# The two heads of a pair as two 64-column products on the two halves of TensorE's array

## The chip, the cores and the metric

The kernel runs on one core of a Trainium2 chip. The metric is the device time of one execution, in microseconds (us). Before the change it is 762.14 us, the median of three runs (761.79, 762.14 and 766.78).

## The reference

Eight sequences of 576 tokens, eight heads of 64 channels each (512 channels), everything in float32:

```python
kv  = einsum('bhsd,bhse->bhde', k, v)          # per head: 64 x 64, summed over 576 tokens
out = einsum('bhsd,bhde->bhse', q, kv)
x   = out / sqrt(mean(out * out) + 1e-6) * g_norm            # heads side by side: [8, 576, 512]
gate = sigmoid(causal convolution of x over 5 tokens)
y1  = (gate * (x @ w_val)) @ w_out
theta = y1 @ w_theta
y   = w_tok_r @ (y1 * cos(theta)) + w_tok_i @ (y1 * sin(theta))
u   = y1 + y
result = u + maximum(u @ w_ch, 0)
```

The change concerns the first line alone: the product of keys and values of each head.

## The kernel before, in words

Work runs in two phases. In the first one the eight sequences go through attention, normalization, convolution and the products with w_val and w_out; in the second one through the angles, the mix over the tokens and the product with w_ch. The big products of both run as three passes over split operands; the products of attention run in plain float32, and the trace shows each such product as two MATMUL instructions with a weight load (LDWEIGHTS) each.

Heads are handled in pairs, four pairs (NP) to a sequence. A pair's keys and values lie in one tile `kv`: 128 tokens on the partitions, five chunks of tokens, 128 columns (head 0, then head 1). The fifth chunk has only 64 tokens, so it fills partitions 0 to 63. Five such buffers exist. `load_kv` issues two DMAs for each, the first four chunks and the 64 tokens of the fifth (lines 143 and 144), on the queue of SyncE (SP), which also issues the other loads of this phase.

`key_value` (line 156) multiplies keys and values of whole pairs: five products of 128 by 128 columns for a pair, added up in a PSUM bank `kvp` (line 162). Of each 128 x 128 result only the two 64 x 64 blocks on the diagonal, one for each head, are wanted; two copies on ScalarE (lines 166 and 167) take them to `bd`, which holds zeros elsewhere. `attention` (line 169) multiplies queries with `bd` (`o`, line 177), sums squares on ScalarE and VectorE (lines 180 to 186), takes the inverse root by Newton steps on VectorE (193 to 199) and scales (`xn`, line 203). `transposes` brings the result to channels over tokens (`xt`, line 218; copies on ScalarE in lines 220 and 221, the low part `xl` on VectorE in line 222), `value` multiplies by w_val (`v`, lines 238 to 240) and by the gate (`g`, `gh`, `gl`), `first` by w_out (`y`, the same lines). `conv` (line 225) is the convolution, on VectorE for the most part. Weights that arrive as doubles are decoded on VectorE and ScalarE (lines 92 to 96) where there is room.

The order of the program text gives priorities to a scheduler, which sets the order of instructions on each engine before the run: an instruction is placed when its operands are due by the scheduler's own reckoning. On the chip each engine then works through its list in that order. From the second sequence on, three pairs of heads (four in one case) of later sequences are multiplied between the end of one sequence's `v` and the next one's transposes (table UNITS, lines 36 and 359 to 372). The first loads of all are in the order of the table START (line 32), as far as the scheduler keeps to it.

Of the kernel before, what the change touches and what calls it, by code (L numbers as in the profile page):

```python
# [12 lines left out]
AF = mybir.ActivationFunctionType  # L13
ALU = mybir.AluOpType

P = 128
B = 8
S = 576
D = 64
DM = 512  # L20
NP = 4          # pairs of heads = chunks of 128 channels
NM = 4
HS = 288        # half of a sequence
PAD = 4
# [5 lines left out]
NBD = 4  # L30
# the order of the first loads: k = keys and values, q = queries (of a pair of heads), v = w_val, o = w_out, c = conv
START = "v0 k0 k1 v1 k2 k3 v2 q0 q1 q2 q3 v3 k4 c0 k5 k6 o0 k7 o1 o2 o3 q4 q5 q6 q7"
WVFIRST = 3      # chunks of w_val decoded before the first normalization
WOFIRST = 2      # chunks of w_out decoded before the second one
LEAD = 3         # sequences whose k^T v runs ahead
UNITS = (0, 3, 3, 3, 3, 4, 0, 0, 0)    # pairs of heads of later ones, with each sequence
YFIRST = 2       # chunks of the first sequence's product with w_out ahead of the second's transposes
EARLY = 2        # chunks of the convolution that run before the gate's product
RATE = (1, 3)    # chunks of weights decoded with a sequence
LATER = 1000     # their priority  # L40
CHFIRST = 2      # chunks of w_ch decoded in the first phase
MIXES = ((8,), (2, 6))      # tiles of the mix that share its stationary operands: first sequence, others
SUMS_ON_VECTOR = (range(5), (2, 4), ())
# the high word of 2**-127 as a double, read as a float32, squared
TINY = (2.0 ** -15 * 1.125) ** 2
# [3 lines left out]
def attention_moe_holo_kernel(ctx, tc, kvm, kvt, qt, gn, w_val, conv_w, w_out, w_th, w_tok, w_ch, outT):  # L49
    """x = rmsnorm(q (k^T v)) g; y1 = (sigmoid(conv x) * (x w_val)) w_out;  # L50
    u = y1 + Wr (y1 cos) + Wi (y1 sin); out = u + relu(u w_ch).

    The weights come as doubles (raw words) and are cut to float32 on the chip. Big products
    run as three float32r passes over exact 12+12-bit parts of both operands."""
    nc = tc.nc
# [9 lines left out]
    def parts(h, l, src):  # L65
        """h + l = src, both exact in float32r."""
        one = nc.scalar.activation(h, src, AF.Copy)  # L67
        return nc.vector.tensor_tensor(l, src, h.bitcast(F32), ALU.subtract), one

    def fetch(pool, src, width, name, tag=""):  # L70
        words = 1 if src.dtype == F32 else 2
        if pool is px:
            raw = pool.tile([P, width if tag else DM, words], I32, tag="raw" + tag, bufs=1 if tag else 3, name=f"raw_{name}")
        else:
            raw = pool.tile([P, DM, words], I32, tag="fT", bufs=2, name=f"raw_{name}")
        raw = raw[:, :width, :]
        # a queue of its own for the one that must not wait behind the loads of the second phase
        queue = nc.gpsimd if pool is not px else nc.sync
        if words == 1:
            raw = raw.bitcast(F32).rearrange("p a w -> p (a w)")  # L80
            queue.dma_start(out=raw, in_=src)
        else:
            queue.dma_start(out=raw, in_=src.bitcast(I32).rearrange("p (a w) -> p a w", w=2))
        return raw

    def decode(pool, raw, width, name, tag=""):
        """Doubles to float32 (toward zero; under 2**-127 to zero)."""
        if raw.dtype == F32:
            return raw
        dst = pool.tile([P, width if tag else DM], F32, tag="dst" + tag if pool is px else "fTt", bufs=(1 if tag else 2) if pool is px else 1, name=f"dst_{name}")[:, :width]  # L90
        lo, hi, d = raw[:, :width, 0], raw[:, :width, 1], dst.bitcast(I32)
        nc.vector.tensor_scalar(d, hi, 0x07FFFFFF, 3, ALU.bitwise_and, ALU.logical_shift_left)
        nc.vector.scalar_tensor_tensor(d, hi, -0x40000000, d, ALU.bitwise_and, ALU.bitwise_or)
        nc.vector.scalar_tensor_tensor(d, lo, 29, d, ALU.logical_shift_right, ALU.bitwise_or)
        nc.scalar.activation(hi.bitcast(F32), hi.bitcast(F32), AF.Square)
        nc.vector.scalar_tensor_tensor(dst, hi.bitcast(F32), TINY, dst, ALU.is_ge, ALU.mult)
        return dst
# [20 lines left out]
    nc.gpsimd.memset(halfpi, 0.5 * math.pi)  # L118
    nc.scalar.activation(halfpi, halfpi, AF.Sigmoid)      # the table of the first phase, early
    nc.gpsimd.memset(halfpi, 0.5 * math.pi)  # L120
# [7 lines left out]

    # ---------------------------------------------------------------- phase 1
    px_stack, py_stack = ExitStack(), ExitStack()  # L130
# [7 lines left out]

    def load_kv(b, pairs=range(NP)):
        kv = []  # L140
        for p in pairs:
            t = px.tile([P, 2, 5, P], F32, tag="kv", bufs=5, name=f"kv{b}_{p}")
            nc.sync.dma_start(out=t[:, :, 0:4, :], in_=kvm[b, p])
            nc.sync.dma_start(out=t[0:D, :, 4, :], in_=kvt[b, p])
            kv.append(t)
        return kv
# [9 lines left out]
    def key_value(b, kv, p0=0):  # L156
        """k^T v of the pairs from p0 on, as blocks on a diagonal"""
        ps = bank(f"kvp{b}_{p0}")
        n = len(kv)
        for p in range(n):  # L160
            for c, (_, r) in enumerate(CH):
                nc.tensor.matmul(ps[:, p * P:(p + 1) * P], kv[p][:r, 0, c, :], kv[p][:r, 1, c, :],  # L162
                                 start=(c == 0), stop=(c == 4))
        bd = bds[b % NBD]
        psv = ps.rearrange("p (a e) -> p a e", a=NP)
        nc.scalar.activation(bd[0:D, p0:p0 + n, 0:D], psv[0:D, :n, 0:D], AF.Copy)
        nc.scalar.activation(bd[D:P, p0:p0 + n, D:P], psv[D:P, :n, D:P], AF.Copy)

    def attention(b, q):
        bd = bds[b % NBD]  # L170
# [3 lines left out]
        for c, (s0, n) in enumerate(CH):  # L174
# [12 lines left out]
            po.append(o)  # L187
        # 1 / sqrt(mean + eps): an estimate from the bits, then three Newton steps
        ssf = ss.rearrange("p c h -> p (c h)")
# [76 lines left out]
    def to_tokens(rows, src, tag, bufs, name):  # L266
        """src: channels (32 i + c, m) over tokens; to rows of tokens, channels in the order (i, m, c)."""
        n = rows.shape[0] // 32
        t = qx.tile([P, n, P], F32, tag=tag, bufs=bufs, name=name)
        for v, (a, w) in src:  # L270
            nc.vector.transpose(t[:, a:a + w // 32, :].rearrange("p j (m c) -> p j m c", m=NM),
                                v.rearrange("p m (j c) -> p j m c", c=32))
        dst = rows.rearrange("(j r) (i x) -> i r j x", r=32, i=4)
        for i in range(4):
            nc.sync.dma_start(out=dst[i], in_=t[32 * i:32 * (i + 1)])
# [16 lines left out]
    def load_tails(b):  # L292
        """The last 64 tokens of two sequences."""
        ft = qx.tile([P, NM, 2, D], F32, tag="ft", bufs=1, name=f"ft{b}")
        for j in range(2):
            nc.sync.dma_start(out=ft[:, :, j, :], in_=ydram[b + j][:, :, DM:S])
        to_tokens(stdram[b // 2], [(ft[:, :, j, :], (2 * j, D)) for j in range(2)], "fTt", 1, f"fTt{b}")
        th = qx.tile([P, NM, P], F32R, tag="th", bufs=1, name=f"th{b}")
        tl = qx.tile([P, NM, P], F32R, tag="tl", bufs=1, name=f"tl{b}")
        parts(th, tl, ft.rearrange("p m j s -> p m (j s)"))  # L300
        yts = []
        for j in range(2):
            t = qx.tile([P, S], F32, tag="tok", bufs=2, name=f"ytt{b}_{j}")[:, :DM]
            for r in range(2):
                nc.sync.dma_start(out=t[r * D:(r + 1) * D], in_=stdram[b // 2][j * D:(j + 1) * D, :])
            yts.append(t)
        return th, tl, yts
# [4 lines left out]
    raw = {}  # L312
# [80 lines left out]

    # ---------------------------------------------------------------- phase 2

# [7 lines left out]
    def theta(name, yh, yl):  # L403
        """f = theta / 2 pi less its nearest integer, and |f|"""
        ps = bank(f"th{name}")
# [33 lines left out]
    def phase_tails(b, th, tl, yts):  # L439
        """Rows 0-63 hold y1 cos, rows 64-127 y1 sin, of a sequence's last 64 tokens."""  # L440
        fr, co = theta(f"t{b}", th, tl)
# [37 lines left out]
    def halves(b, then=None):  # L479
        """z of sequence b"""  # L480
        nonlocal tls, zt
# [78 lines left out]
```

## Time and profile before

| | |
|---|---|
| median of three runs | 762.14 us |
| span of the profiled execution, first to last instruction | 760.7 us |
| TensorE matmul (PE) busy | 743.6 us, 98% of the span |
| TensorE weight loads (PEld) busy | 712.0 us, 94% |
| VectorE (DVE) | 535.2 us, 70% |
| ScalarE (ACT) | 391.6 us, 51% |
| GpSimd (POOL) | 6.6 us, 1% |
| line 162, the product of keys and values | 320 matmuls, 51.3 us busy, first at 8.1 us, last at 252.8 us |

No time of its own is listed for the profiled execution; its span lies 1.4 us under the median of the runs. Times in the rows are microseconds from the start of the span, durations too unless they say ns. A matmul's duration holds its way through the array, so matmuls overlap: the pace of TensorE is read from the distance between starts, not from durations. `L162` is line 162 of the kernel before. Granted clock 1.00 is TensorE's upper level (2.4 GHz), 0.50 its lower one (1.2 GHz).

### The profile page before, as it was taken

To read this page: it belongs to the slowest core of one execution; us is meant where nothing else is said; L and a number is where in the kernel's file an instruction comes from. 1 tells how busy PE (TensorE), PEld (TensorE's weight loads), DVE (VectorE), ACT (ScalarE), POOL (GpSimd) and SP (SyncE) were. 2 spreads that over 40 slices of the span, in tenths; PEclk is the share of its full clock that TensorE was granted. 3 is DMA by queue.
4 is the path that set the end of the run, shared out by engine and by line. 5 is a ranking of instruction groups with operands and counts; after the bars stand their busy time and mean duration, and the time that the engine had idled before them with its cause. 6 is when DMAs were issued, how large, how long until landed. Compare 5 with 4: busy or idle time off the path is not lost.

```text
span 760.7 us, 13908 instructions
## 1 busy us (share of the span) xinstructions
PE 743.6 (98%) x5264; PEld 712.0 (94%) x5264; DVE 535.2 (70%) x1045; ACT 391.6 (51%) x1173; POOL 6.6 (1%) x32
## 2 busy tenths in 40 slices
PE   5899999999999999999999999999999999999998
PEld 4789999999999999989899899899999999998997
DVE  4898897979798889868883772953863934836504
ACT  2565968777777677467441550631631613614301
POOL 1000000000000000000000000000000000000000
PEclk9999999999999999999999999999999999999999
DMA  9969635545444034743527034063042161160101
GB/s 300 313 202 272 217 117 171 166 164 175 169 136 150 32 105 126 216 133 97 164 75 217 1 120 117 9 173 110 17 142 79 57 167 55 55 173 9 63 2 62
DMA packets 77539, 97.53 MB, mean 128 GB/s; under 512 B 11168, under 2 KB 50208, under 8 KB 77472
## 3 DMA queue, kind: packets, MB, share of 16 engines
q1 hardware_dynamic: 76896, 94.55, 40.5%
q0 software_dynamic: 576, 2.10, 0.8%
q8 instruction: 41, 0.67, 0.4%
q14 instruction: 26, 0.21, 0.1%
HBM read 65.66 MB, written 30.97 MB: 127 GB/s over the span
## 4 chain that ended last, share of the span: by engine, by line
PE 94%; ACT 2%; DMA 2%; DVE 1%; SPq 1%; issue 0%; DVEq 0%; ACTq 0%
PE u L461 10%; PE u L463 10%; PE u L462 10%; PE kvp L162 5%; PE y L238 5%; PE v L238 5%; PE y L239 5%; PE v L239 4%; PE y L240 4%; PE c L238 4%; PE c L240 4%; PE c L239 4%; PE v L240 4%; PE o L177 4%; PE th L409 3%; PE th L408 3%
## 5 line engine op out<-in xcount | busy, mean ns | idle before, releaser
L466 DVE TENSOR_TENSOR f<-u,f 128x288 f32<-128x288 f32 x64 | 26.5, 454 | 128.1 <-PE u L463 128.1
L67 ACT ACTIVATE uh<-f 128x288 fp32r<-128x288 f32 x64 | 26.2, 444 | 150.4 <-DVE f L466 150.4
L229 DVE SCALAR_TENSOR_TENSOR acc<-x,cw,acc 128x576 f32<-128x576 f32 x128 | 95.7, 812 | 3.2 <-ACT acc L227 3.2
L238 PE MATMUL y<-gh,woh 128*128 128x288 f32 x256 | 76.3, 299 | 0.0
L238 PE MATMUL v<-xh,wvh 128*128 128x288 f32 x256 | 76.3, 299 | 0.0
L239 PE MATMUL v<-xh,wvl 128*128 128x288 f32 x256 | 75.7, 296 | 0.0
L239 PE MATMUL y<-gh,wol 128*128 128x288 f32 x256 | 75.6, 296 | 0.0
L238 PE MATMUL c<-uh,wch 128*128 128x288 f32 x256 | 75.4, 295 | 0.0
L240 PE MATMUL c<-ul,wch 128*128 128x288 f32 x256 | 75.4, 295 | 0.0
L239 PE MATMUL c<-uh,wcl 128*128 128x288 f32 x256 | 75.4, 294 | 0.0
L240 PE MATMUL v<-xl,wvh 128*128 128x288 f32 x256 | 75.3, 294 | 0.0
L240 PE MATMUL y<-gl,woh 128*128 128x288 f32 x256 | 75.0, 294 | 0.0
L162 PE MATMUL kvp<-kv 128*128 128x128 f32 (+1 forms) x320 | 51.3, 304 | 10.1 <-DMA kv<-in_kvm_dram 8.7
L162 PEld LDWEIGHTS kvp<-kv 128*128 128x128 f32 (+1 forms) x320 | 43.3, 201 | 17.2 <-DMA kv<-in_kvm_dram 9.8
L185 ACT ACTIVATE junk<-o 128x64 f32<-128x64 f32 (+1 forms) x264 | 55.0, 250 | 4.4 <-PE o L177 3.8
L185 ACT ACTIVATION_READ_ACCUMULATOR junk<-o 128x1 f32 (+1 forms) x264 | 53.8, 233 | 0.0
L409 PE MATMUL th<-wth,yl 128*128 128x512 f32 x128 | 50.2, 393 | 0.0
L407 PE MATMUL th<-wth,yh 128*128 128x512 f32 x128 | 50.1, 391 | 0.0
L408 PE MATMUL th<-wtl,yh 128*128 128x512 f32 x128 | 50.0, 391 | 0.0
L238 PEld LDWEIGHTS v<-xh,wvh 128*128 128x128 f32 x256 | 48.0, 188 | 1.1 <-ACT junk L185 0.9
L238 PEld LDWEIGHTS y<-gh,woh 128*128 128x128 f32 x256 | 48.0, 188 | 0.7
L239 PEld LDWEIGHTS c<-uh,wcl 128*128 128x128 f32 x256 | 48.0, 188 | 0.3
(188 smaller groups left out, 2146.5 us busy)
## 6 DMA issues: line engine op xcount, KB each, us to landing
kv<-in_kvm_dram SPq DMA_DIRECT2D x32, 512.0 KB, 6.6
q<-in_qt_dram SPq DMA_DIRECT2D x32, 288.0 KB, 5.3
yd<-yo SPq DMA_DIRECT2D x64, 144.0 KB, 1.8
f<-yd SPq DMA_DIRECT2D x32, 288.0 KB, 3.8
out_dram<-f SPq DMA_DIRECT2D x64, 144.0 KB, 1.8
sd<-fT SPq DMA_DIRECT2D x64, 128.0 KB, 2.5
yt<-sd SPq DMA_DIRECT2D x8, 1024.0 KB, 5.4
raw_tk<-in_w_tok_dram SPq DMA_DIRECT2D x10, 512.0 KB, 6.2
```

Of the source, the lines that this page charges most:

```text
L162: nc.tensor.matmul(ps[:, p * P:(p + 1) * P], kv[p][:r, 0, c, :], kv[p][:r, 1, c, :], start=(c == 0), stop=(c == 4))
L185: nc.scalar.activation(junk[:n], o[:n, h * D:(h + 1) * D], AF.Square, scale=0.125, accum_out=ss[:n, c, h:h + 1])
L229: nc.vector.scalar_tensor_tensor(a, x[:, m, k:k + S], cw[:, m * 5 + k:m * 5 + k + 1], a, ALU.mult, ALU.add)
L238: nc.tensor.matmul(ps[:, :HS], wh[:, m, ks], xh[:, k, tsl], start=(k == 0), stop=False)
L239: nc.tensor.matmul(ps[:, :HS], wl[:, m, ks], xh[:, k, tsl], start=False, stop=False)
L240: nc.tensor.matmul(ps[:, :HS], wh[:, m, ks], xl[:, k, tsl], start=False, stop=(k == 3))
L407: nc.tensor.matmul(ps, yh[:, k, :], wth[0][:, k, :], start=(k == 0), stop=False)
L408: nc.tensor.matmul(ps, yh[:, k, :], wth[1][:, k, :], start=False, stop=False)
L409: nc.tensor.matmul(ps, yl[:, k, :], wth[0][:, k, :], start=False, stop=(k == 3))
L461: nc.tensor.matmul(ps[:, :HS], zh[:, ms], wkh[:, j, sl], start=(i == 0), stop=False)
L462: nc.tensor.matmul(ps[:, :HS], zh[:, ms], wkl[:, j, sl], start=False, stop=False)
L463: nc.tensor.matmul(ps[:, :HS], zl[:, ms], wkh[:, j, sl], start=False, stop=(i == 8))
```

## The change

Each chunk of tokens now gives two products instead of one: 64 columns of head 0's keys with 64 columns of its values, placed on columns 0 to 63 of the array, and the same of head 1 on columns 64 to 127 (`tile_position`). The results lie in 64 partitions each, side by side, and only the wanted blocks are computed. Partitions 64 to 127 of the fifth chunk are filled with zeros by GpSimd ahead of the loads, in every use of a buffer, and the fifth chunk is multiplied over all 128 rows. So 160 products (320 matmul instructions) of 128 x 128 columns become 320 products (640 instructions) of 64 x 64 columns, and 32 fills of 64 partitions x 256 elements are added. The copies to `bd` read the new places. Other lines of the diff only drop comments; line numbers move by one from line 143 on and by four from line 169 on.

```diff
@@ def load_kv @@
             t = px.tile([P, 2, 5, P], F32, tag="kv", bufs=5, name=f"kv{b}_{p}")
+            nc.gpsimd.memset(t[D:P, :, 4, :], 0.0)
             nc.sync.dma_start(out=t[:, :, 0:4, :], in_=kvm[b, p])
             nc.sync.dma_start(out=t[0:D, :, 4, :], in_=kvt[b, p])
...
@@ def key_value @@
         for p in range(n):
-            for c, (_, r) in enumerate(CH):
-                nc.tensor.matmul(ps[:, p * P:(p + 1) * P], kv[p][:r, 0, c, :], kv[p][:r, 1, c, :],
-                                 start=(c == 0), stop=(c == 4))
+            for c in range(5):
+                for j in range(2):
...
+                    js = slice(j * D, (j + 1) * D)
+                    nc.tensor.matmul(ps[js, p * D:(p + 1) * D], kv[p][:, 0, c, js], kv[p][:, 1, c, js],
+                                     start=(c == 0), stop=(c == 4), tile_position=(0, j * D))
         bd = bds[b % NBD]
-        psv = ps.rearrange("p (a e) -> p a e", a=NP)
-        nc.scalar.activation(bd[0:D, p0:p0 + n, 0:D], psv[0:D, :n, 0:D], AF.Copy)
-        nc.scalar.activation(bd[D:P, p0:p0 + n, D:P], psv[D:P, :n, D:P], AF.Copy)
+        psv = ps[:, 0:n * D].rearrange("p (a e) -> p a e", a=n)
+        nc.scalar.activation(bd[0:D, p0:p0 + n, 0:D], psv[0:D], AF.Copy)
+        nc.scalar.activation(bd[D:P, p0:p0 + n, D:P], psv[D:P], AF.Copy)
```

The scheduler places some work anew. The first place is the start of the program on SP's queue; `raw_wv` are chunks of w_val, `kv_0` to `kv_3` the first sequence's pairs of heads, `q_0` to `q_3` its queries. Before:

```order
L83 DMA raw_wv_117<-in_w_val_dram 128x1024
L143 DMA kv_0_119<-in_kvm_dram 128x2x512
...
L143 DMA kv_1_122<-in_kvm_dram 128x2x512
...
L83 DMA raw_wv_125<-in_w_val_dram 128x1024
L143 DMA kv_2_127<-in_kvm_dram 128x2x512
...
L143 DMA kv_3_130<-in_kvm_dram 128x2x512
...
L83 DMA raw_wv_133<-in_w_val_dram 128x1024
L152 DMA q_0_135<-in_qt_dram 128x576
L152 DMA q_1_137<-in_qt_dram 128x576
L152 DMA q_2_139<-in_qt_dram 128x576
L152 DMA q_3_141<-in_qt_dram 128x576
```

With the change:

```order
L83 DMA raw_wv_117<-in_w_val_dram 128x1024
L144 DMA kv_0_119<-in_kvm_dram 128x2x512
...
L83 DMA raw_wv_127<-in_w_val_dram 128x1024
L83 DMA raw_wv_137<-in_w_val_dram 128x1024
L153 DMA q_0_139<-in_qt_dram 128x576
L153 DMA q_1_141<-in_qt_dram 128x576
L153 DMA q_2_143<-in_qt_dram 128x576
L144 DMA kv_1_123<-in_kvm_dram 128x2x512
...
L144 DMA kv_2_129<-in_kvm_dram 128x2x512
...
L144 DMA kv_3_133<-in_kvm_dram 128x2x512
...
L153 DMA q_3_145<-in_qt_dram 128x576
```

Three of the first sequence's four pairs of heads are now asked for behind the second and third chunk of w_val and three of the queries.

The second place is TensorE where the third and fourth sequence's products of keys and values are spread over the first one's product with w_out (`y`). Before, the fourth sequence's first pair is followed by ten rows of `y`:

```order
L162 MATMUL kvp_0_700<-kv_0_571 128x128 x5
L238 MATMUL y_0_0_723<-gh_399,woh 128x288
L239 MATMUL y_0_0_723<-gh_399,wol 128x288
L240 MATMUL y_0_0_723<-gl_400,woh 128x288
...
L238 MATMUL y_0_0_723<-gh_399,woh 128x288
L162 MATMUL kvp_0_700<-kv_1_574 128x128 x5
```

With the change, by two:

```order
L166 MATMUL kvp_0_779<-kv_0_623 64x64 x10
L242 MATMUL y_0_0_822<-gh_451,woh 128x288
L242 MATMUL y_0_1_838<-gh_451,woh 128x288
L166 MATMUL kvp_0_779<-kv_1_627 64x64 x10
L243 MATMUL y_0_0_822<-gh_451,wol 128x288
```

The second pair's product has moved up by eight rows of `y`; the third and fourth pair's stand a few rows later than before. In the first sequence's `o` TensorE now goes chunk by chunk of tokens, where it went query by query. From the second sequence on the three pairs stand where they stood, behind the last row of `v` and ahead of the transposes.

## Rows read from the trace of the kernel before

**Rows 1.** Section 1 of the page: busy time, share of the span, instructions.
```profile
PE 743.6 (98%) x5264; PEld 712.0 (94%) x5264; DVE 535.2 (70%) x1045; ACT 391.6 (51%) x1173; POOL 6.6 (1%) x32
```

**Rows 2.** Section 4 of the page: the chain that ended last, shares by engine.
```profile
PE 94%; ACT 2%; DMA 2%; DVE 1%; SPq 1%; issue 0%; DVEq 0%; ACTq 0%
```

**Rows 3.** Timeline, PE, two later stretches: start, length, line, output<-input, shape, count.
```profile
98.81 4.48 PE L162 MATMUL kvp<-kv 128*128 128x128 f32 x30
103.21 2.36 PE L218 MATMUL xt<-ident,xn 128*128 128x128 f32 x20
...
247.07 5.98 PE L162 MATMUL kvp<-kv 128*128 128x128 f32 x40
252.98 2.36 PE L218 MATMUL xt<-ident,xn 128*128 128x128 f32 x20
```

**Rows 4.** Timeline, weight loads, single ones of the first of these blocks.
```profile
98.81 0.19 PEld L162 LDWEIGHTS kvp<-kv 128*128 128x128 f32 x1
...
99.48 0.19 PEld L162 LDWEIGHTS kvp<-kv 128*128 128x128 f32 x1
...
99.79 0.18 PEld L162 LDWEIGHTS kvp<-kv 64*128 64x128 f32 x1
...
100.20 0.19 PEld L162 LDWEIGHTS kvp<-kv 128*128 128x128 f32 x1
```

**Rows 5.** Timeline, weight loads of 64 columns (o), and of 64-row transposes (xt).
```profile
84.63 0.19 PEld L177 LDWEIGHTS o<-bd,q 128*128 128x128 f32 x1
84.94 0.13 PEld L177 LDWEIGHTS o<-bd,q 128*64 128x64 f32 x1
85.00 0.14 PEld L177 LDWEIGHTS o<-bd,q 128*64 128x64 f32 x1
...
85.65 0.14 PEld L177 LDWEIGHTS o<-bd,q 128*64 128x64 f32 x1
85.96 0.19 PEld L238 LDWEIGHTS v<-xh,wvh 128*128 128x128 f32 x1 [0.17 <-issue]
...
105.11 0.32 PEld L218 LDWEIGHTS xt<-ident,xn 64*128 64x128 f32 x4 [0.17 <-issue]
```

**Rows 6.** Timeline, PE and DVE, the start of the program.
```profile
15.17 1.57 PE L162 MATMUL kvp<-kv 128*128 128x128 f32 x10 [0.26 <-DMA kv<-in_kvm_dram]
17.71 4.83 PE L177 MATMUL o<-bd,q 128*128 128x128 f32 x40 [0.96 <-ACT bd L167]
...
21.51 3.05 DVE L181 TENSOR_REDUCE ss<-sq 128x8 f32<-128x512 f32 x5 [0.90 <-ACT sq L180]
...
27.30 3.08 DVE L203 TENSOR_TENSOR xn<-o,y 128x512 f32<-128x512 f32 x5
...
28.14 1.50 PE L218 MATMUL xt<-ident,xn 128*128 128x128 f32 x9 [1.99 <-DVE xn L203]
...
33.74 0.40 PE L238 MATMUL v<-xh,wvh 128*128 128x288 f32 x1
```

**Rows 7.** Windows: stretch, length, busy time by engine, granted clock, DMA share, GB/s.
```profile
12.54:17.70 5.16, 3.80 (x24) 2.88 (x24) 3.32 (x6) 2.06 (x4) 0.00 (x0) 1.00 1.04 360
29.61:33.02 3.41, 3.41 (x16) 2.96 (x15) 3.41 (x7) 1.79 (x4) 0.00 (x0) 0.50 1.01 342
```

**Rows 8.** Timeline, PE and DVE, the last early pair; the second sequence's normalization and transposes.
```profile
67.89 1.47 PE L162 MATMUL kvp<-kv 128*128 128x128 f32 x10
...
70.23 3.08 DVE L203 TENSOR_TENSOR xn<-o,y 128x512 f32<-128x512 f32 x5
...
72.58 2.30 PE L218 MATMUL xt<-ident,xn 128*128 128x128 f32 x20
```

**Rows 9.** DVE in later sequences: timeline row; waits from 112 to 223 us (total, times, longest).
```profile
99.47 3.07 DVE L203 TENSOR_TENSOR xn<-o,y 128x512 f32<-128x512 f32 x5
...
DVE g L251 <- PE v L240: 7.4, 6, 1.6
```

**Rows 10.** Timeline, POOL: a fill of 128 x 512 elements.
```profile
0.91 0.52 POOL L136 MEMSET bd<- 128x512 f32 x1
```

## The prediction

> **What bounds the kernel now.** I read the shares of busy time first, then the chain of waits, then single starts in the timeline. TensorE is busy for 98% of the span [rows 1] and holds 94% of the chain that ended last [rows 2]: what TensorE is spared, the program is spared, wherever nothing else is late in its place. So the question is what a block of key-value products takes on TensorE, read from starts. A block of three pairs begins at 98.81 and the transposes behind it at 103.21: 4.40 us for 30 instructions; the one of four pairs takes 252.98 - 247.07 = 5.91 us for 40 [rows 3]. There are four blocks of three pairs and one of four between 75 and 255 us: 4 x 4.40 + 5.91 = 23.5 us for 16 of the 32 pairs. The other 16 lie before 75 us, where other things set the pace (below).
>
> **What is in a block.** Between 98.81 and 99.48 lie six loads' steps, 0.11 us each [rows 4]: a 128-column load, beside the running product. The fifth chunk breaks the step. From the last load over 128 rows to the first over 64 it is 0.31 us, and from that, two instructions on, to the next over 128 rows 0.41 us instead of 0.22 [rows 4]. So a 64-row product costs about 0.39 us over its plain step; 4.40 is 30 x 0.11 = 3.35 and three times 0.35, in agreement. The array empties before it is used in another shape.
>
> **The change, part by part.**
>
> *The zero fill* removes that: all products run over 128 rows, so about 0.35 us a pair goes.
>
> *Entering and leaving the 64-column shape* comes in its place, once a block. The last tokens' `o` are such products now: from the last 128-column load to the first of 64 columns 0.31 us (84.63 to 84.94), and at the way out again 0.31 (85.65 to 85.96), where 0.11 is plain [rows 5]. Two changes of shape at 0.20: 0.40 us a block.
>
> *The products.* 60 instructions in place of 30 in a block of three. A 64-column load is followed by the next after 0.055 us (84.94 to 85.00), and four 64-column transposes with their loads start 0.06 us apart (the fourth load ends 0.32 after the first began, and one lasts 0.14) [rows 5]. So one after the other an instruction takes about 0.058 us. If the two halves of the array work at once, two fit into that time: 0.029. No row shows two products at once, so these are my two ends, and a third, slow one is below. I take 0.029, and this is the choice on which the forecast hangs. The reason is how loads wait in the rows: a load begins the moment the product before it begins (a load and a product both at 98.81) [rows 3, 4], which reads as waiting until the cells' spare weights have been taken over. For the other half of the columns these are other cells, whose spare weights are free a step earlier; the data moves through other columns; and the shape stays the same, so nothing need empty. Row for row the nearest value is 0.058, which is why the other case keeps a good third of the chances.
>
> With 0.029 a block of three takes 0.40 + 60 x 0.029 = 2.14 us, one of four 0.40 + 80 x 0.029 = 2.72; together 11.3 in place of 23.5: **-12.2 us**. With 0.058: 3.88 and 5.04, together 20.6: -2.9 us.
>
> The Trainium skill ("TensorEngine Tiling (Array Packing)", Tiling Modes, Key Properties) says that a change of the tiling mode drains the array but a change of tile does not, and that tiles can load and multiply in parallel; the drain agrees with 0.31 us in [rows 5], the parallel work no row here shows. By it the sum would be the -12.2 us.
>
> *What becomes late instead.* With a block of 2.14 us the transposes come at about 101.0 instead of 103.2. They need `xn`, five instructions from 99.47 to 102.54, one every 0.61 us [rows 9]: the first four are ready when their transposes (0.45 us a chunk) come, the fifth just so. VectorE's slack in a sequence is what it waits for TensorE's `v`: 7.4 us in three sequences, 2.5 each [rows 9], against 2.3 us saved in each. That is nearly all of it, so I give back a tenth: **+1.2 us**.
>
> *The start.* Behind the new order of loads the first sequence's last pair lands later: ahead of it now also stand one chunk of w_val (512 KB) and three queries (288 KB each), 1.4 MB, at 360 GB/s [rows 7] 3.9 us. It landed for 15.17; now about 19, and `o` starts at 21.6 instead of 17.71, because its operand needs all four pairs. `o` takes 4.8 us, then come the sums (five, last done at 24.56), the root, `xn` at 27.30 and the transposes at 28.14 [rows 6]. Since `o` now comes chunk by chunk, its last sum ends about 0.7 us sooner after it, so `xn` moves by some 3.2 us. Of that about 1.4 us comes back: before, a pair's product stands between the transposes, at the granted clock of 0.50 [rows 7], and makes 5.6 us of the way from the first transpose to `v` (28.14 to 33.74) [rows 6]; now the transposes follow each other. This leaves about 1.8. Against this, TensorE's 16 early pairs get shorter too, but this stretch hardly gains: the next transposes start at 72.58 and their `xn` run from 70.23 to 73.31, so at most a microsecond can come off there [rows 8]; and the fourth sequence's second pair, moved up by eight rows of `y`, makes TensorE wait for that load with `y` behind it. Idle time may also cost the clock: after the wait ahead of 28.14 the granted clock falls to 0.50 for 3.4 us [rows 6, 7], and a longer pause between loads can do this ahead of `o`, up to 2 us. Altogether **+1.5 us**, between 0 and 4.5.
>
> *The fills* cost nothing: a fill twice as wide over twice the partitions takes 0.52 us on GpSimd [rows 10], which is idle for 99% of the span [rows 1]. Each stands between a buffer's release and its DMA; in later sequences loads have a whole sequence's time ((247.07 - 98.81) / 4 = 37.07 us from one block to the next [rows 3]), which covers it. Without that cover, at most 0.5 us for each of the three pairs loaded just ahead of their use there, the last at 67.89 [rows 8], inside the +1.5. The copies to `bd` keep size and number.
>
> **Sum.** -12.2 + 1.2 + 1.5 = -9.5 us. The profiled execution's span is 760.7 us, 1.4 under the median of 762.1; against the median: 752.6, I say **753 us**.
>
> **Rivals.**
>
> *One after the other* (the change does not do what it says: the halves take turns). For it: every product in the rows starts a step after the one before, and each instruction's load is put behind the product before it. -2.9 + 1.5 gives 760.7, 757 to 766 with the start's bounds. Chance 0.34, cases in between included.
>
> *Loads no longer hidden.* If the load for one half may not run beside a product on the other half, an instruction takes load and product in turn, 0.055 + 0.058 = 0.113 us. A block of three takes 0.40 + 60 x 0.113 = 7.2 us, one of four 9.4: 38.2 in place of 23.5, +14.7; the third and fourth sequence's 8 pairs, the last at 67.89 [rows 8], add 0.8 each, of which half may hide, +3; with the start +1.5: 781 us. It decides against the change from about half of each load uncovered on (320 instructions x 0.03 = 9.6, which beats the 2.9). Against it: in [rows 5] loads of 64 columns do run beside the product on the same columns. The Trainium skill ("TensorE: Matmul & The Clock Gate", Part 3, What overlaps and what doesn't) has such a rule: loads overlap running products only on other row groups, and here both halves use all rows. By that rule the change would be slower; the 0.11 us steps in [rows 4], with all rows on both sides, do not bear it out. Chance 0.10.
>
> *Each change of half empties the array*, as each change of shape does. Then 30 changes x 0.20 come to a block of three and 40 to the one of four: 16 pairs x 10 x 0.20 = 32 over the -2.9, some 8 more before 75 us: about 800 us. Chance 0.06.
>
> **Range and chances.** The forecast, chance 0.50, runs from 748 (no slack lost, start at 0 and a microsecond gained at 72 us) to 758 (0.035 an instruction, start +4.5). With the second case the range is 748 to 768; the slow cases, 0.16, and a little at the edges stay out. A measurement of this kernel tells about 1% (7.6 us) from no change. The forecast lies just beyond it: of its 0.50 I count 0.34 as faster and 0.16 as same; of the second case 0.02 faster, 0.30 same, 0.02 slower; the slow cases slower. Faster 0.36, same 0.46, slower 0.18.
>
> **What would show it.** In the timeline, the block behind the second sequence's `v` from its first product to the transposes: 2.1 us is the forecast, 3.9 taking turns, 7 loads uncovered, 10 emptying at each change. Starts of products on the two halves nearly together in pairs would show them at once. No break of 0.3 us should be left inside a block, and one at either end. At the start `o` should begin near 21.6 and the transposes near 31. The period from block to block, 37 us now, should fall to 34.8; if the block shrinks but the period does not, VectorE is the bound and the wait of the transposes names `xn`. The forecast is wrong above all if the two halves share what a load or a product needs.

## The result, and the profile after

The change takes 755.45 us (median of four runs, 754.04 to 757.18); the kernel before, run beside it, 762.91 (four runs, 761.79 to 766.78). The ratio is 0.9888, its 95% interval 0.9857 to 0.9919: 1.1% faster, 7.5 us. The forecast was 753.

The profiled execution of the change took 757.18 us with a span of 755.4, so it is the slowest of the four. Against the profiled execution of before (span 760.7) it gains 5.3 us. They fall into three stretches, cut at the first later block of key-value products and at the transposes behind the last one:

| stretch | before | change | difference | forecast |
|---|---|---|---|---|
| start to the first later block | 98.81 | 104.60 | +5.8 | +1.5 |
| from there to the transposes behind the last block | 154.17 | 142.39 | -11.8 | -11.0 |
| from there to the end | 507.7 | 508.4 | +0.7 | 0 |

The page of the change, shares of busy time (section 1) and its chain of waits by engine (section 4):

```profile
PE 726.1 (96%) x5584; PEld 697.9 (92%) x5584; DVE 534.8 (71%) x1045; ACT 391.7 (52%) x1173; POOL 16.4 (2%) x64
...
PE 88%; DMA 4%; ACT 4%; DVE 3%; issue 0%; SPq 0%; POOL 0%; DVEq 0%; ACTq 0%; POOLq 0%
```

TensorE has 320 instructions more and is busy for 17.5 us less than in [rows 1]. Only 5.3 of them reach the span, and TensorE's share of the chain falls from 94% [rows 2] to 88%: the rest became waiting, for DMAs, ScalarE and VectorE.

The later blocks of the change, timeline of PE:

```profile
104.60 1.97 PE L166 MATMUL kvp<-kv 128*64 128x64 f32 x60
106.67 2.90 PE L222 MATMUL xt<-ident,xn 128*128 128x128 f32 x20
...
139.97 1.97 PE L166 MATMUL kvp<-kv 128*64 128x64 f32 x60
141.87 2.35 PE L222 MATMUL xt<-ident,xn 128*128 128x128 f32 x20
...
244.51 2.55 PE L166 MATMUL kvp<-kv 128*64 128x64 f32 x80
246.99 2.36 PE L222 MATMUL xt<-ident,xn 128*128 128x128 f32 x20
```

From a block's first product to the transposes it now takes 2.07 us once and 1.90 three times, where it took 4.40 [rows 3], and 2.48 in place of 5.91 for four pairs. The period from block to block is 35.4, 34.6, 35.0 and 35.0 us, where it was 37.07.

The same line, seen through four short windows that open at 104.65 and close at 104.70, 104.75, 104.81 and 104.87. A row's count is of the products that have begun by the window's end:

```profile
104.60 0.28 PE L166 MATMUL kvp<-kv 128*64 128x64 f32 x2
...
104.60 0.34 PE L166 MATMUL kvp<-kv 128*64 128x64 f32 x4
...
104.60 0.39 PE L166 MATMUL kvp<-kv 128*64 128x64 f32 x6
...
104.60 0.45 PE L166 MATMUL kvp<-kv 128*64 128x64 f32 x8
```

Two more products for each step of 0.058 us: they begin in pairs. The starts in the trace read 104.706 and 104.712, 104.764 and 104.771, 104.822 and 104.829, and so on through the block: 6 to 7 ns apart, then the next pair.

The start of the program of the change, timeline of PE, DVE and POOL:

```profile
3.83 1.58 POOL L143 MEMSET kv<- 64x256 f32 x5
...
15.13 1.34 PE L166 MATMUL kvp<-kv 128*64 128x64 f32 x20 [7.08 <-DMA kv<-in_kvm_dram]
...
21.20 6.70 PE L181 MATMUL o<-bd,q 128*128 128x128 f32 x39 [0.93 <-ACT bd L171]
...
32.20 3.07 DVE L207 TENSOR_TENSOR xn<-o,y 128x512 f32<-128x512 f32 x5
...
32.95 4.29 PE L222 MATMUL xt<-ident,xn 128*128 128x128 f32 x20 [3.20 <-DVE xn L207]
...
70.90 0.80 PE L166 MATMUL kvp<-kv 128*64 128x64 f32 x20
...
77.78 2.75 PE L222 MATMUL xt<-ident,xn 128*128 128x128 f32 x20 [1.77 <-DVE xn L207]
```

And two of its stretches (length, busy time by engine, granted clock, DMA share, GB/s):

```profile
32.15:42.39 10.24, 9.44 (x56) 8.88 (x57) 8.97 (x16) 7.34 (x14) 0.31 (x1) 0.50 0.35 131
...
66.28:69.69 3.41, 3.41 (x16) 3.41 (x15) 2.02 (x7) 0.41 (x2) 0.41 (x2) 0.50 0.94 320
```

In [rows 6] `o` takes 4.83 us; here 6.70. A pair's products take 1.34 us before 20 us and 0.80 at 70.90. At 32.15, in the wait of 3.20 us ahead of the transposes, the granted clock falls to 0.50 and stays there for 10.24 us; before the change it was 3.41 us [rows 7]. At 66.28 it falls again.

### The profile page after: what moved, and what is told of

It reads as the page before. It is cut to its first block, busy times and chain, and to the rows that moved or that the text cites. A ratio compares the mean times of both kernels' runs of the same rounds, so it can differ in the third digit from the quotient of the medians.

```text
span 755.4 us, 14634 instructions
## 1 busy us (share of the span) xinstructions
PE 726.1 (96%) x5584; PEld 697.9 (92%) x5584; DVE 534.8 (71%) x1045; ACT 391.7 (52%) x1173; POOL 16.4 (2%) x64
## 4 chain that ended last, share of the span: by engine, by line
PE 88%; DMA 4%; ACT 4%; DVE 3%; issue 0%; SPq 0%; POOL 0%; DVEq 0%; ACTq 0%; POOLq 0%
PE u L467 10%; PE u L466 10%; PE u L465 10%; PE c L244 4%; PE c L242 4%; PE c L243 4%; PE v L242 4%; PE y L242 4%; PE o L181 4%; PE v L243 4%; PE y L243 4%; PE v L244 4%; PE y L244 4%; PE th L413 3%; PE th L411 3%; PE th L412 3%
## 5 line engine op out<-in xcount | busy, mean ns | idle before, releaser
L243 PEld LDWEIGHTS v<-xh,wvl 128*128 128x128 f32 x256 | 48.9, 191 | 0.0
L243 PEld LDWEIGHTS y<-gh,wol 128*128 128x128 f32 x256 | 48.8, 191 | 0.1
L244 PEld LDWEIGHTS v<-xl,wvh 128*128 128x128 f32 x256 | 48.8, 191 | 0.0
```

Of the source, the lines that this page charges most:

```text
L243: nc.tensor.matmul(ps[:, :HS], wl[:, m, ks], xh[:, k, tsl], start=False, stop=False)
L244: nc.tensor.matmul(ps[:, :HS], wh[:, m, ks], xl[:, k, tsl], start=False, stop=(k == 3))
```

## Experiments

Times are medians; each ratio is to the kernel before as it ran beside that kernel (median 762.91 us beside the change, 763.3 beside the next four, 763.67 beside the last four). "Later block" is the start of the first one in the profiled execution. The profiled execution is not always the typical one: that of the change is the slowest of its four (757.18 us), that of the halves without fill the fastest of its four (753.42).

| kernel | us | ratio, 95% interval | later block | a block of three |
|---|---|---|---|---|
| the change | 755.45 | 0.9888, 0.9857 to 0.9919 | 104.60 | 1.90 |
| fill behind the DMAs | 753.36 | 0.9854, 0.9829 to 0.9879 | 101.01 | 1.90 |
| before, with the new order of loads | 767.11 | 1.0040, 1.0018 to 1.0061 | 102.60 | 4.40 |
| halves in turn | 758.69 | 0.9933, 0.9907 to 0.9959 | 103.56 | 2.75 |
| fill only, full products | 757.25 | 0.9906, 0.9882 to 0.9931 | 99.33 | 3.35 |
| halves, no fill | 755.55 | 0.9906, 0.9883 to 0.9928 | 97.87 | 2.63 |
| full products early | 751.37 | 0.9839, 0.9824 to 0.9854 | 99.50 | 2.18 |
| change and extra products | 759.42 | 0.9944, 0.9932 to 0.9957 | 106.80 | 1.90 |
| full early, fill behind the DMAs | 748.66 | 0.9801, 0.9787 to 0.9815 | 97.39 | 1.90 |

The block of three is the first one in the profiled execution; for the change, whose first took 2.07 us, one of the other three. The 2.18 us of full products early hold a wait for `xn`.

### Do the two halves work at once?

Halves in turn: all chunks of one head, then all of the other.

```diff
-            for c in range(5):
-                for j in range(2):
+            for j in range(2):
+                for c in range(5):
```

> The change with the loops over halves and chunks exchanged: all five chunks of head 0, then all five of head 1, so ten instructions in a row go to one half of the array. Theory (the halves work at once only because their instructions alternate; instructions begin in order): 0.058 us an instruction, a block of three pairs 3.7 to 3.9 us, some 9 to 10 us over the change: 764 to 766 us. Rival (each half has a queue of its own that runs far ahead): the block stays at 1.9 to 2.1 us and the time at 754 to 757.

Measured: a block of 2.75 us, four pairs 3.56, which neither theory gave; the time, 758.69 us, lies between theirs too. The block of this kernel, then windows that open at 103.65 and close at 103.955, 104.07, 104.18, 104.24 and 104.35 (timeline, PE):

```profile
103.56 2.82 PE L166 MATMUL kvp<-kv 128*64 128x64 f32 x60
106.31 2.36 PE L222 MATMUL xt<-ident,xn 128*128 128x128 f32 x20
...
103.56 0.56 PE L166 MATMUL kvp<-kv 128*64 128x64 f32 x6
...
103.56 0.68 PE L166 MATMUL kvp<-kv 128*64 128x64 f32 x9
...
103.56 0.80 PE L166 MATMUL kvp<-kv 128*64 128x64 f32 x13
...
103.56 0.85 PE L166 MATMUL kvp<-kv 128*64 128x64 f32 x14
...
103.56 0.97 PE L166 MATMUL kvp<-kv 128*64 128x64 f32 x16
```

Up to 103.955 one product starts per 0.058 us; then about two (9 to 13 within 0.11 us); then one again (14 to 16 within 0.11). A head has ten instructions here. So within a half the step is 0.058, and around each change of half some three instructions of the next one run beside the last of this one. The two ends of the forecast, 0.058 and 0.029, stand side by side in one block, and what decides between them is whether a product for the other half lies near enough in the queue. The instruction that signals a pair's end, by the program text its 20th, is the 23rd to start: the next pair's first ones have passed it.

The Trainium skill ("TensorEngine Tiling (Array Packing)", Tiling Modes, Key Properties) says that tiles load and multiply in parallel; starts 6 to 7 ns apart in the change agree. The Trainium skill ("TensorE: Matmul & The Clock Gate", Part 3, The mechanism) says in its list of what overlaps that loads overlap products only on other row groups and that products start in program order; the change's pairs, each on all 128 rows, and the 23rd start here do not bear either out.

### What are the fill and the split worth apart?

Fill only: the change with one 128 x 128 product a chunk, over filled rows.

```diff
-                for j in range(2):
...
-                    nc.tensor.matmul(ps[js, p * D:(p + 1) * D], kv[p][:, 0, c, js], kv[p][:, 1, c, js],
-                                     start=(c == 0), stop=(c == 4), tile_position=(0, j * D))
+                nc.tensor.matmul(ps[:, p * P:(p + 1) * P], kv[p][:, 0, c, :], kv[p][:, 1, c, :],
+                                 start=(c == 0), stop=(c == 4))
...
```

> The zero fill alone: full products of 128 x 128 columns over 128 rows in all five chunks, fill and load order as in the change. Theory: no break of 0.3 us is left in a block; three pairs take 30 x 0.1115 = 3.35 us, four 4.46, together 5.7 us less than before in the later blocks; at the start some 4 to 6 us are lost to the order of loads: 761 to 763 us. Rival (the breaks come from something else than the 64 rows, such as the end of an accumulation): blocks stay at 4.4 us, 766 to 768.

The block came out as expected. Timeline of PE:

```profile
20.68 4.86 PE L178 MATMUL o<-bd,q 128*128 128x128 f32 x40 [0.86 <-ACT bd L168]
...
30.47 2.90 PE L219 MATMUL xt<-ident,xn 128*128 128x128 f32 x20 [1.39 <-DVE xn L204]
...
99.33 3.51 PE L163 MATMUL kvp<-kv 128*128 128x128 f32 x30
102.68 2.30 PE L219 MATMUL xt<-ident,xn 128*128 128x128 f32 x20
```

3.35 us = 30 x 0.111: no break is left. The five blocks together shrink from 23.5 to 17.9 us by the fill; the split takes them on to 10.25. The time was lower than expected because this kernel, with the change's order of loads, starts its later blocks at 99.33 and not at 104.60. That turned the question to the start.

Halves, no fill: the fifth chunk over 64 rows again.

```diff
-            nc.gpsimd.memset(t[D:P, :, 4, :], 0.0)
...
-            for c in range(5):
+            for c, (_, r) in enumerate(CH):
...
-                    nc.tensor.matmul(ps[js, p * D:(p + 1) * D], kv[p][:, 0, c, js], kv[p][:, 1, c, js],
+                    nc.tensor.matmul(ps[js, p * D:(p + 1) * D], kv[p][:r, 0, c, js], kv[p][:r, 1, c, js],
```

> The change without the zero fill: two halves, but the fifth chunk over 64 rows, loads in the order of the kernel before. Theory (each change of shape empties the array, 0.2 us more than a step): a block of three pairs has two changes a pair inside it, 60 x 0.029 + 0.40 + 5 or 6 x 0.2 = 3.1 to 3.4 us against 1.9 with the fill; some 5 us are lost in the later blocks and some 2 gained at the start by the order: 756 to 759 us. Rival (64 rows of the same column halves need no emptying): 1.9 to 2.1 us a block and 751 to 754.

Timeline of PE:

```profile
97.87 2.70 PE L165 MATMUL kvp<-kv 128*64 128x64 f32 x60
100.50 2.35 PE L221 MATMUL xt<-ident,xn 128*128 128x128 f32 x20
```

Windows of the same kernel:

```profile
26.06:32.89 6.83, 4.70 (x35) 4.17 (x36) 6.42 (x20) 3.79 (x7) 0.00 (x0) 0.50 0.85 290
```

2.63 us (97.87 to 100.50), below the expected 3.1 to 3.4 and above the rival's 2.1: a 64-row chunk costs less between halves, but it costs. The fill is worth 0.73 us a block of three here and 1.06 between full products. The median, 755.55 us, lies just under what was expected.

### What made the start late?

The order of the first loads alone, in the kernel before:

```diff
-START = "v0 k0 k1 v1 k2 k3 v2 q0 q1 q2 q3 v3 k4 c0 k5 k6 o0 k7 o1 o2 o3 q4 q5 q6 q7"
+START = "v0 k0 v1 v2 q0 q1 q2 k1 k2 k3 q3 v3 k4 c0 k5 k6 o0 k7 o1 o2 o3 q4 q5 q6 q7"
```

> The kernel before with nothing but the first loads in the order that the change brought: two chunks of w_val and three queries ahead of the second to fourth pair. Theory (order): o begins at 21 to 22 us instead of 17.7, the first transposes at 31 to 33, the first later block 4 to 6 us later than 98.8, and the time is 766 to 768 us. Rival (clock): the full products keep TensorE busy enough between loads to hold the upper clock, and the order alone costs 1 to 2 us: 763 to 764.

Timeline of PE:

```profile
23.00 4.83 PE L177 MATMUL o<-bd,q 128*128 128x128 f32 x40 [1.01 <-ACT bd L167]
...
32.76 2.81 PE L218 MATMUL xt<-ident,xn 128*128 128x128 f32 x20 [0.42 <-DVE xn L203]
...
102.60 4.48 PE L162 MATMUL kvp<-kv 128*128 128x128 f32 x30
```

The order costs 3.8 us by the medians (767.11 - 763.3; the interval of the ratio allows 1.4 to 4.7) and 3.8 in the profile (102.60 - 98.81): the time is in the order theory's range, the later block just under its 4 to 6 us. The other way round, the change with the fill asked for behind the two DMAs, which gives the first loads their old order back:

```diff
-            nc.gpsimd.memset(t[D:P, :, 4, :], 0.0)
             nc.sync.dma_start(out=t[:, :, 0:4, :], in_=kvm[b, p])
             nc.sync.dma_start(out=t[0:D, :, 4, :], in_=kvt[b, p])
+            nc.gpsimd.memset(t[D:P, :, 4, :], 0.0)
```

> The change with one line moved: a buffer's zero fill is issued behind its two DMAs, and the first loads are in the order of the kernel before again. Theory (the change gives some 11.8 us in the later blocks and loses 5.8 at the start, most of it by the new order of loads): the later blocks stay at 1.9 to 2.1 us, the first transposes move from 32.9 us back to 28 to 29, the first later block begins at 98 to 100 instead of 104.6, and the time is 750 to 751 us. Rival (the loss at the start comes from TensorE's lower clock, since its short products no longer keep it busy between loads, whatever the order): the later blocks begin at 102 or later, and the time is 753 to 756.

Timeline of PE:

```profile
16.58 7.63 PE L181 MATMUL o<-bd,q 128*128 128x128 f32 x39 [0.93 <-ACT bd L171]
...
29.72 2.82 PE L222 MATMUL xt<-ident,xn 128*128 128x128 f32 x12 [4.23 <-DVE xn L207]
...
101.01 1.97 PE L166 MATMUL kvp<-kv 128*64 128x64 f32 x60
```

Windows of the same kernel:

```profile
29.49:32.90 3.41, 3.18 (x20) 2.85 (x22) 3.29 (x7) 2.03 (x4) 0.00 (x0) 0.50 0.85 313
...
73.86:77.27 3.41, 3.41 (x18) 2.89 (x16) 3.13 (x6) 3.41 (x7) 0.00 (x0) 0.50 0.61 210
```

Between the two theories: `o` starts 1.1 us earlier than before the change and yet the later block 2.2 us later. Part of the loss is not the order. `o` takes 7.63 us where it took 4.83, and the clock falls at two places.

Next, full products over filled rows for the first four sequences only, halves for the later ones, in the change's order of loads:

```diff
+        if b <= LEAD:
+            for p in range(n):
+                for c in range(5):
+                    nc.tensor.matmul(ps[:, p * P:(p + 1) * P], kv[p][:, 0, c, :], kv[p][:, 1, c, :],
+                                     start=(c == 0), stop=(c == 4))
...
+            return
```

> The change with full products of 128 x 128 columns (over zero-filled rows) for the first four sequences, the halves only from the fifth on; fill and load order as in the change. Theory (the change's loss ahead of the later blocks is TensorE's clock: its short products leave it idle between loads and the granted clock is low until 25 us and again at 32 to 42 and 66 to 70): the clock holds from some 19 us on as in the fill-only kernel, the first later block begins at 99 to 100 us instead of 104.6, the later blocks take 1.9 to 2.1 us, and the time is 748 to 750.5 us, against 755.5 of the change and 757.3 of the fill alone. Rival (the start is lost to the order of loads or to the fills, and VectorE then bounds the later sequences): first later block at 103 or later, or the later periods stay over 35.5 us; 752 to 756.

Timeline of PE:

```profile
21.46 4.86 PE L191 MATMUL o<-bd,q 128*128 128x128 f32 x40 [0.86 <-ACT bd L169]
...
31.25 2.90 PE L232 MATMUL xt<-ident,xn 128*128 128x128 f32 x20 [1.39 <-DVE xn L217]
...
99.50 1.97 PE L176 MATMUL kvp<-kv 128*64 128x64 f32 x60
...
136.43 1.39 PE L176 MATMUL kvp<-kv 128*64 128x64 f32 x40 [0.66 <-DVE g L265]
```

Windows of the same kernel:

```profile
19.84:99.50 79.66, 73.67 (x575) 70.03 (x573) 70.17 (x151) 56.25 (x213) 4.71 (x18) 1.00 0.75 236
```

Longer products, an earlier end: 751.37 us, 4.1 less than the change. `o` starts at the same time (21.46 against 21.20) but takes 4.86 us instead of 6.70; the clock stays at 1.00 from 19.84 on; the later block starts 5.1 us sooner. The time lies a microsecond above what was expected; the second later block waits 0.66 us for VectorE's `g`, whose slack the earlier start has used up.

If the clock is the reason, other work on TensorE should do as well. The change, with five full products a pair more that nobody reads, for the first four sequences:

```diff
+            if b <= LEAD:
+                for c in range(5):
+                    nc.tensor.matmul(ps[:, NP * D:NP * D + P], kv[p][:, 0, c, :], kv[p][:, 1, c, :],
+                                     start=(c == 0), stop=(c == 4))
```

> The change, and behind each pair's products in the first four sequences five more full products of the same operands into columns of the bank that nobody reads: 80 products more than the change, some 18 us of added TensorE time at the upper clock. Theory (clock): the added work keeps the granted clock up in the first 45 us, and the first later block begins no later than in the change, at 99 to 103 us against 104.6; 750 to 755 us. Rival (added work on a bound engine costs what it takes, less what waits hide): the first later block at 107 or later, 758 us or more.

Timeline of PE:

```profile
57.87 0.80 PE L166 MATMUL kvp<-kv 128*64 128x64 f32 x20 [0.74 <-DVE g L259]
58.60 1.38 PE L170 MATMUL kvp<-kv 128*128 128x128 f32 x10
...
72.91 1.38 PE L170 MATMUL kvp<-kv 128*128 128x128 f32 x10
...
106.80 1.97 PE L166 MATMUL kvp<-kv 128*64 128x64 f32 x60
```

In the profiled execution the clock stayed at 1.00 from 18.85 us on, and still the kernel lost 4 us by the medians, as the rival had it: eight pairs with their extra products stand in one row from 57.87 to 74.01, 16.2 us on the path, and each pair pays the way into another shape and out. This run shows that the clock can be held by work; it doesn't show what that is worth.

Last, both cures together, full products early and the fill behind the DMAs:

```diff
-            nc.gpsimd.memset(t[D:P, :, 4, :], 0.0)
             nc.sync.dma_start(out=t[:, :, 0:4, :], in_=kvm[b, p])
             nc.sync.dma_start(out=t[0:D, :, 4, :], in_=kvt[b, p])
+            nc.gpsimd.memset(t[D:P, :, 4, :], 0.0)
...
+        if b <= LEAD:
...
+            return
```

> As the kernel with full products in the first four sequences, and the zero fill behind the DMAs, which brings the first loads back into the order of the kernel before. Theory (with the clock held, the order of loads costs a microsecond or less, since the normalization's chain and VectorE set the pace behind it): first later block at 98 to 99.5 us, 747.5 to 750 us, within 1.5 us of the other. Rival (the order costs 3 to 5 us by itself): 3 us or more under the other.

Timeline of PE:

```profile
17.34 4.83 PE L191 MATMUL o<-bd,q 128*128 128x128 f32 x40 [0.95 <-ACT bd L169]
...
97.39 1.97 PE L176 MATMUL kvp<-kv 128*64 128x64 f32 x60
```

748.66 us, the fastest of all: 2.0% under the kernel before, 6.8 us under the change. The old order of loads is worth 2.7 us here, between what the two theories gave. The later blocks start 1.4 us sooner than in the kernel before.

## Why the prediction was right, and where it was not

**The products at 0.029 us.** Right, and shown twice: by the pairs of starts, and by the halves in turn, where the same instructions fall back to 0.058 when their partner is out of reach. The reason given, that the other half's spare weights are free a step earlier, fits both but was not tested by itself. Of the two readings that gave 0.058, only that of `o` is one of 64-column loads: the four transposes in [rows 5] load 128 columns over 64 rows. The halves in turn confirm the number.

**Entering and leaving the shape, 0.40 us a block.** Too dear. The way in, from the last product of `v` to the first of the block, is 104.38 to 104.60, 0.22 us where 0.13 is plain; out it is 0.15 where 0.06 is plain. The measured 1.90 us, from the first product to the transposes, hold the way out but not the way in; with it a block takes 1.99 where the forecast had 2.14. The five blocks shrank by 13.3 us (23.5 to 10.25), less 0.09 for each way in, 12.8 in place of 12.2.

**The zero fill, 0.35 us a pair.** Right: full products over filled rows take 3.35 us in place of 4.40. Its other side, that the fills cost nothing, holds for their time: 0.31 us each (1.58 for five, overlapping ends included), and GpSimd is busy for 2%. But where the fill stands in the program text is what gave the loads their new order, and that cost 2 to 4 us.

**VectorE's slack, +1.2.** Right in size. From the first transpose behind a block to the product that follows the transposes, summed over four blocks, it was 9.14 us and is now 10.30: +1.16, as at 106.67, where they take 2.90 us because `xn` is late. VectorE's wait for `v` in the three sequences of [rows 9] has shrunk from 7.4 us to

```profile
DVE g L255 <- PE v L244: 3.2, 3, 1.1
```

in the change (total, times, longest). A faster start eats the rest, as the 0.66 us in the kernel with full products early shows.

**The start, +1.5 us, between 0 and 4.5.** This is the step that failed: +5.8 in the profiled execution. `o` was forecast for 21.6 and came at 21.20, so the first link, the loads, was right. The forecast then had the transposes near 31 and 1.4 us coming back behind them; they came at 32.95 and ran at half the clock for 4.29 us. What I allowed for the clock, "up to 2 us", inside a sum that took no more than a part of it, was too small. The runs divide the 5.8 in three steps. From before to full products early with the old order, 98.81 to 97.39, it is -1.4: up to there TensorE, VectorE and ScalarE run the same instructions in the same order, and what differs is the fills and the early blocks without breaks. The new order of loads, to 99.50, is +2.1; the short form of the early products, to 104.60, +5.1. By the medians the last two steps are +2.7 (748.66 to 751.37) and +4.1 (751.37 to 755.45); with the old order the short form costs +4.7 (748.66 to 753.36). By the ratios to the kernels before that ran beside them, the short form costs 3.7 and 4.0.

Up to the second sequence's `o` the rows put the price of the short form down to the clock. Timeline of PE, `o` in the change in windows that open at 21.3 and close at 24.10, 25.25 and 26.40, and `o` of the halves in turn:

```profile
21.20 3.14 PE L181 MATMUL o<-bd,q 128*128 128x128 f32 x13 [0.93 <-ACT bd L171]
...
21.20 4.33 PE L181 MATMUL o<-bd,q 128*128 128x128 f32 x19 [0.93 <-ACT bd L171]
...
21.20 5.45 PE L181 MATMUL o<-bd,q 128*128 128x128 f32 x29 [0.93 <-ACT bd L171]
...
21.07 4.86 PE L181 MATMUL o<-bd,q 128*128 128x128 f32 x40 [0.92 <-ACT bd L171]
```

Six starts in 1.15 us, then ten in the next 1.15: single starts lie 0.21 us apart up to 25.20 and 0.11 from 25.37 on, and 25.32 is where the change's first recorded granted clock, 1.00, begins. In the kernel with full products early the record begins at 19.84, ahead of `o`, which goes at 0.11 throughout. Then come the 10.24 us at 0.50: from the first transpose to `v` it is 5.49 us (32.95 to 38.44), with full products early 3.97 (31.25 to 35.22). The second sequence's `o` starts 3.4 us later than there (53.04 against 49.67).

The other 1.7 us come behind that, and here the clock is not the only thing that differs. With the shorter products the scheduler also placed some work otherwise on TensorE, VectorE and ScalarE than with full products early, most of it from 46 us on, so this step does not change one thing alone. The clock falls again at 66.28; VectorE waits 2.0 us for ScalarE's `woh`, which it does not in the kernel with full products early, and `xn` comes late for the second transposes (1.77 us at 77.78). No run separates these. The halves in turn have the change's order on all of these engines and the clock at 1.00 from 18.52; their `o` keeps its pace, their second `o` is 1.0 us behind full products early (50.70), and still their first later block is 4.1 us behind (103.56), with two falls of 3.41 us at 32.17 and 76.55. So a slow `o` is not needed for most of the loss, and that the clock is all of it is not shown.

The executions of one kernel speak for the clock. The four of the change have mean granted clocks of 0.991, 0.993, 0.995 and 0.999 and times of 757.18, 756.29, 754.61 and 754.04; those of the halves without fill 0.988, 0.992, 0.994 and 0.995 and 758.38, 756.41, 754.70 and 753.42. With the fill behind the DMAs there is no such order. The profiled one of the change lost most, so the start typically costs a microsecond or two less than +5.8. The fastest execution of the change, at 0.999, is still 2.7 us above the median with full products early. The mean does not count a slow start: half of the two falls (10.24 + 3.41 us) in 755.4 us gives the 0.991 by itself, and nothing is recorded before 25.32. So the 2.7 us may lie there, or in the scheduler's order. The Trainium skill ("TensorE: Matmul & The Clock Gate", Part 1, HAM oscillation) tells of a loop in which the clock falls in every wait for the next load. The trace agrees in part: the fall at 32.15 lies in a wait, but one for VectorE's `xn`, and that at 66.28 behind three waits (0.90, 0.67 and 0.81 us), of which only the last is for a load.

The halves without fill and the kernel with the fill behind the DMAs have the same order on TensorE, VectorE and ScalarE, and the former start their later block 3.1 us sooner (97.87 against 101.01). The clock's record begins at 1.00 at 19.23 in the one and at 22.66 in the other; `o`, begun within 0.15 us of each other, ends 1.7 us sooner (22.32 against 24.05). The first fall is the longer one there (6.83 us against 3.41), but there is no second fall, which in the other kernel costs 1.0 us at the second transposes (3.68 us to the product behind them against 2.68). So the short form has no fixed price at the start. By the medians the halves without fill are 2.2 us the slower of the two: the profiled execution is the one in four with the mildest clock.

**Early pairs gain nothing.** Right, and too mild: with the order that the scheduler chose, shorter products there are a loss.

**The last stretch, forecast at nothing, +0.7.** One wait in the second phase, which the kernel before does not have; whether it makes all of the 0.7, no run isolates. Timeline of PE in the change:

```profile
340.18 0.40 PE L465 MATMUL u<-wkh,zht 128*128 128x288 f32 x1 [1.05 <-DVE fr L416]
```

The rivals fell. Taking turns would have shown 3.9 us a block, loads uncovered 7, emptying at each change 10; 1.90 was seen. In profiled executions the sum was off by -0.8 in the later blocks, +4.3 in the start and +0.7 at the end, 4.2 in all; by the medians, with the change's milder executions, by 2.5.

## What to carry to other kernels

Products that need only half of the array's columns can run two at once when instructions for the two halves alternate; the same instructions in runs of ten lose about half of that (2.75 us a block, between 1.90 and some 3.7 at one start per 0.058 us). Where TensorE waits for loads, shorter products won nothing here, and the granted clock was lower for the stretch behind: keep the long form there and use the short one where TensorE is the bound. An instruction that costs nothing on its own engine can still move a scheduler's order of loads; read the queue, not only the engine. And a kernel that differs in one line can differ in the order of every engine: compare the orders before a difference is put down to that line.

## What was not expected of the hardware

- Instructions for the two halves overlap across a change of half for about three instructions, and start out of the program's order there: a pair's 20th is the 23rd to start.
- The way from a 128-column to a 64-column shape costs 0.09 us beside the plain step in these blocks, not the 0.20 read from the kernel before.
- Less work for TensorE, with the order that came with it, made the program later: 99.50 us to the first later block with full early products, 104.60 with halves.
- Executions of one kernel can differ along with the granted clock: 753.42 us at a mean granted clock of 0.995, 758.38 at 0.988, for the halves without fill.
